# A first product on four PSUM bank pairs, half of v's first cast on GpSimd ahead of the weight loads, and two units of chunk 1 in another order

## Chip, cores, metric

One core of one Trainium2 chip. The metric is the device time of one execution in microseconds (us). The kernel before takes 262.2 to 262.4 us (median, in every set of rounds). The experiments come from three chips, one for each set of rounds, each beside runs of the kernel before on the same chip; so kernels of different sets are compared by their ratios to it.

## The reference, cut to what matters

```python
# per batch and head: q softmaxed over its 64 columns, k over its 576 rows
kv  = einsum('bhsd,bhse->bhde', k_s, v)
x   = einsum('bhsd,bhde->bhse', q_s, kv)      # -> x: 4608 x 512
h   = x @ w_in                                 # 512 -> 2048
out = (h * sigmoid(h)) @ w_out                 # 2048 -> 512
```

q, k and v are [8, 8, 576, 64], the output is 4608 x 512, all float32.

## The kernel before

Tokens go in chunks of 512 (the first product of chunk 0 takes the 576 of batch 0). In front of chunk 0 stands a short chain for batch 0: exponential, sum and normalisation of q, transposes on TensorE, exponential of k, cast of v, k times v ("kv"), the product with transposed q that gives XT, and its evacuation. The first product of chunk 0 (W1 times XT, "wide" in the code) has 16 blocks of 128 rows, each of eight matmuls of 288 columns; its result lies in a pair of PSUM banks until ScalarE (tanh) and VectorE have read it. A block can start only when its pair has been freed.

```python
    def wide_mm(fb, cs, ns=range(2)):
        for c in cs:
            for n in ns:
                nc.tensor.matmul(out=PS[:, 2 * (fb % 3) + n, 0:S // 2],   # pairs 0, 2, 4 in turn
                                 lhsT=W1[:, c, fb*128:(fb+1)*128],
                                 rhs=XTS[0][:, c, n*(S//2):(n+1)*(S//2)], ...)
```

The start of batch 0, and the order in which GpSimd issues its loads (it casts the weights to fp16 in the DMA):

```python
    exp_q(0, 0); qsum(0, 0); exp_q(0, 1)
    nc.gpsimd.tensor_copy(gate, st[0]["kt", 0][0:1, 1, 0:1])   # one element: holds the loads until k has landed
    load_w1(0, 4, 0, 2); load_w1(0, 4, 2, 4); load_w1(4, 8)
    load_w1(8, 16, 0, 2); load_w1(8, 16, 2, 4)
    load(1, "qt", ...) x2; load_w2(0, 4); load(1, "kt", ...) x2; load_w2(4, 8); load(1, "vt", ...) x2
    ...
    vcast(0, 0, nc.scalar)             # v's first half of batch 0, fp32 -> bf16
    trcopy(0, 0, 0, 5, 0, nc.scalar)   # transposed q out of PSUM
```

After the first product come units in a fixed order, the "plain" second product of chunk 0 (`mm2_plain`, "b") mixed with groups of chunk 1's first product (`group`, "g", seven products in the order 1, 2, 6, 5, 7, 4, 3). Work for other engines is tied to the number of a unit and is queued in front of it:

```python
    four_pairs = "ggbgbgbgbbgbgb"
    units += [b0.pop(0) for _ in range(9)]
    units += [{"b": b0, "g": gs}[x].pop(0) for x in four_pairs]        # b1 + 9 and on
    ...
    plan(b1 + 10, lambda: exp_q(2, 0))                                  # ScalarE
    plan(b1 + 11, lambda: (qsum(2, 0, 0), qsum(2, 0, 1), qnorm(2, 0, nc.gpsimd)))   # VectorE, GpSimd

    # in group(t, g, i), behind the matmuls:
        if i == 1:   group_snap(t, 0)     # ScalarE copies banks 0 and 1
        elif i == 2: group_add(t, 0)      # VectorE adds banks 6 and 7: group 5 writes these next
```

The softmax here doesn't subtract the row's maximum and nothing guards it: scores larger than these inputs give would overflow.

Of the kernel before, what the change touches and what calls it, by code (L numbers as in the profile page):

```python
# [17 lines left out]
def kernel(  # L18
# [9 lines left out]
    nc = tc.nc  # L28
    B, H, S, D = q.shape
# [3 lines left out]
    J = S // P  # L33
    NG = H // 2
    NC = DM // 128
# [36 lines left out]
    gate = glob.tile([1, 1], FP32, name="gate")  # L72
    dummy = glob.tile([1, 1], FP32, name="dummy")
    PS = ps.tile([128, 8, 512], FP32, name="PS")
# [10 lines left out]
    st = [dict() for _ in range(B)]  # L85

    def copy(eng, o, i):
        if eng is nc.scalar:
            eng.copy(out=o, in_=i)  # L89
        else:  # L90
            eng.tensor_copy(o, i)  # L91

    def load(b, name, src, cc, eng):
        t = ld.tile([128, 2, J * D], FP32, name=name)
        st[b][name, cc] = t
        x = src[b].rearrange("(g r) (p j) d -> g (r p) (j d)", r=2, j=J)
        eng.dma_start(out=t, in_=x.rearrange("g x y -> x g y")[:, 2 * cc:2 * cc + 2, :])

    def jgd(b, name, cc):
        return st[b][name, cc].rearrange("p g (j d) -> p j g d", d=D)  # L100
# [4 lines left out]
    def exp_q(b, cc, g0=0, g1=2):  # L105
        if "eq" not in st[b]:
            st[b]["eq"] = ap.tile([128, J, NG * D], BF16, name="eq")
        nc.scalar.activation(  # L108
            out=half(st[b]["eq"], cc)[:, :, g0:g1], in_=jgd(b, "qt", cc)[:, :, g0:g1], func=ACT.Exp
        )  # L110

    def exp_k(b, cc):
        nc.scalar.activation(out=half(ek, cc), in_=jgd(b, "kt", cc), func=ACT.Exp)  # L113

    def vcast(b, cc, eng, g0=0, g1=2):
        o = vaug[:, :, 2 * cc + g0:2 * cc + g1, 0:D]
        i = jgd(b, "vt", cc)[:, :, g0:g1, :]
        copy(eng, o, i)
# [21 lines left out]
    def qsum_end(b, cc):  # L140
        new_zq(b)
        nc.vector.reduce_sum(out=st[b]["zq"][:, cc], in_=st[b]["t2", cc], axis=AX.X)
        nc.vector.reciprocal(out=st[b]["rzq"][:, cc], in_=st[b]["zq"][:, cc])
# [16 lines left out]
    def qnorm(b, cc, eng):  # L160
        e = half(st[b]["eq"], cc)
        r = st[b]["rzq"][:, cc]
        eng.tensor_tensor(  # L163
            out=e, in0=e, in1=r[:, :, :, None].to_broadcast([128, J, 2, D]), op=ALU.mult
        )

    def new_qt(b):
        if "qT" not in st[b]:
            st[b]["qT"] = ap.tile([128, J, 2, 128], BF16, name="qT", bufs=2)
        return st[b]["qT"]  # L170
# [7 lines left out]
    def tr(b, cc, j0, j1, bank):  # L178
        t = PS[:, bank, :].bitcast(BF16)
        for j in range(j0, j1):  # L180
            nc.tensor.transpose(
                out=t[:, (j - j0) * 128:(j - j0 + 1) * 128],
                in_=st[b]["eq"][:, j, cc * 128:(cc + 1) * 128],
                identity=ident,
            )

    def trcopy(b, cc, j0, j1, bank, eng=nc.vector):
        t = PS[:, bank, :].bitcast(BF16)[:, 0:(j1 - j0) * 128].rearrange("x (j y) -> x j y", y=128)
        copy(eng, new_qt(b)[:, j0:j1, cc, :], t)

    def kv(b, cc):
        for j in range(J):
            for r in range(2):
                for s in range(2):
                    nc.tensor.matmul(  # L195
                        out=PS[s * 64:(s + 1) * 64, 6 + r, cc * 128:cc * 128 + E1],
                        lhsT=ek[r * 64:(r + 1) * 64, j, (2 * cc + s) * D:(2 * cc + s + 1) * D],
                        rhs=vaug[r * 64:(r + 1) * 64, j, 2 * cc + s, :],
                        start=(j == 0),
                        stop=(j == J - 1),  # L200
                    )
# [28 lines left out]
    def xt_mm(b, cc, col, n, bank, dst):  # L230
        for r in range(2):
            for s in range(2):
                h = slice(s * 64, (s + 1) * 64)
                nc.tensor.matmul(  # L234
                    out=PS[r * 64:(r + 1) * 64, bank + s, dst:dst + n],
                    lhsT=kvn[b % 3][h, cc, r, :],
                    rhs=st[b]["qT"][h, col // P:(col + n) // P, cc, r * 64:(r + 1) * 64],
                )

    def xt_evac(t, cc, bank, d0, d1, o0, eng):  # L240
        o = XTS[t % 2][:, 2 * cc:2 * cc + 2, o0:o0 + d1 - d0]
        copy(eng, o, PS[:, bank:bank + 2, d0:d1])
# [8 lines left out]
    def silu(t, fb, i, o, w):  # L251
        sg = mp.tile([128, S], FP32, name="sg", bufs=3)
        s = sg[:, 0:w]
        if len(i.shape) == 3:
            s = s.rearrange("p (a n) -> p a n", a=2)
        nc.scalar.activation(out=s, in_=i, func=ACT.Tanh, scale=OS)  # L256
        nc.vector.scalar_tensor_tensor(  # L257
            out=o, in0=s, scalar=1.0, in1=i, op0=ALU.add, op1=ALU.mult
        )

    def wide_mm(fb, cs, ns=range(2)):
        for c in cs:
            for n in ns:
                nc.tensor.matmul(  # L264
                    out=PS[:, 2 * (fb % 3) + n, 0:S // 2],
                    lhsT=W1[:, c, fb * 128:(fb + 1) * 128],
                    rhs=XTS[0][:, c, n * (S // 2):(n + 1) * (S // 2)],
                    start=(c == 0),
                    stop=(c == NC - 1),
                )  # L270

    def wide_silu(fb):
        bank = 2 * (fb % 3)
        silu(
            0, fb, PS[:, bank:bank + 2, 0:S // 2],
            GTS[0][:, fb, :].rearrange("p (a n) -> p a n", a=2), S,
        )
# [12 lines left out]
    def mm1(t, fb, bank):  # L290
        o0 = pieces(t)[0][3]
        mm1_mm(t, fb, bank, range(NC))
        nc.scalar.activation(
            out=GTS[t % 2][:, fb, o0:TCH], in_=PS[:, bank, o0:TCH], func=ACT.Silu, scale=1.0 / XS
        )
# [113 lines left out]
    def mm2_plain(t, fc):  # L409
        for tb in range(4):  # L410
            nc.tensor.matmul(  # L411
                out=PS[:, 2 + tb, :],
                lhsT=GTS[t % 2][:, fc, tb * 128:(tb + 1) * 128],
                rhs=W2[:, fc, :],
                start=(fc == 0),
                stop=(fc == NFB - 1),
            )
# [128 lines left out]
    def heat(n, bank=5):  # L546
        for _ in range(n):
            nc.tensor.matmul(out=PS[:, bank, :], lhsT=warm[:, 0:128], rhs=warm, start=True, stop=True)

    def load_w1(f0, f1, c0=0, c1=NC):  # L550
        nc.gpsimd.dma_start(
            out=W1[:, c0:c1, f0 * 128:f1 * 128],
            in_=w_in[c0 * 128:c1 * 128, f0 * 128:f1 * 128].rearrange("(c p) f -> p c f", p=128),
        )
# [8 lines left out]
    exp_q(0, 0)  # L563
    qsum(0, 0)
    exp_q(0, 1)
    nc.gpsimd.tensor_copy(gate, st[0]["kt", 0][0:1, 1, 0:1])
    load_w1(0, 4, 0, 2)
    load_w1(0, 4, 2, 4)
    load_w1(4, 8)
    load_w1(8, 16, 0, 2)  # L570
    load_w1(8, 16, 2, 4)
    load(1, "qt", q, 0, nc.gpsimd)
    load(1, "qt", q, 1, nc.gpsimd)
    load_w2(0, 4)
# [10 lines left out]
    tr(0, 0, 5, J, 1)  # L585
    heat(7)
    qnorm(0, 1, nc.vector)
    vcast(0, 0, nc.scalar)
    trcopy(0, 0, 0, 5, 0, nc.scalar)
    trcopy(0, 0, 5, J, 1)  # L590
    kv(0, 0)
    kvcopy(0, 0, 1)
# [3 lines left out]
    xt_mm(0, 0, 0, 320, 4, 0)  # L596
    xt_mm(0, 0, 320, 256, 0, 0)
    heat(3, 6)
    vcast(0, 1, nc.scalar, 0, 1)
    vcast(0, 1, nc.vector, 1, 2)  # L600
    trcopy(0, 1, 0, 5, 2, nc.scalar)
    trcopy(0, 1, 5, J, 3)
    kv(0, 1)
    kvcopy(0, 1, 2)
    heat(2, 3)
# [2 lines left out]
    xt_mm(0, 1, 0, 320, 6, 0)  # L608
    xt_mm(0, 1, 320, 256, 2, 0)
    wide_mm(0, (0, 1))  # L610
    xt_evac(0, 1, 6, 0, 320, 0, nc.scalar)
    xt_evac(0, 1, 2, 0, 256, 320, nc.vector)
    wide_mm(1, (0, 1))


    units = []
    at = {}

    def plan(u, f):
        at.setdefault(u, []).append(f)  # L620

    def wide(fb):
        wide_mm(fb, range(2 if fb < 2 else 0, NC))
        wide_silu(fb)

    for fb in range(NFB):
        units.append(lambda fb=fb: wide(fb))
# [17 lines left out]
    four_pairs = "ggbgbgbgbbgbgb"  # L645

    b0 = [lambda i=i: mm2_plain(0, i) for i in range(NFB)]
    gs = [lambda i=i: group(1, 1, i, None, True) for i in ORDER]
    units += [b0.pop(0) for _ in range(9)]
    units += [{"b": b0, "g": gs}[x].pop(0) for x in four_pairs]  # L650
    units += [lambda i=i: mm1(1, FB[i], i % 4) for i in range(HF)]
    assert not (b0 or gs)

# [34 lines left out]
    for t in range(2, NCH):  # L688
# [5 lines left out]
        gs = [lambda t=t, g=g, i=i: group(t, g, i) for g in (1, 0) for i in ORDER]  # L694
# [72 lines left out]
    b1 = begin[1]  # L767
# [4 lines left out]
    plan(13, lambda: (exp_q(1, 1, 1, 2), qsum_pair(1, 1), qnorm(1, 0, nc.gpsimd)))  # L772
    plan(14, lambda: (load(2, "qt", q, 0, nc.gpsimd), load(2, "qt", q, 1, nc.gpsimd)))
    plan(b1 + 2, lambda: (exp_k(1, 0), exp_k(1, 1)))
    plan(b1 + 3, lambda: (tr(1, 0, 0, 5, 6), tr(1, 0, 5, J, 7)))
    plan(b1 + 3, lambda: (trcopy(1, 0, 0, 5, 6, nc.scalar), trcopy(1, 0, 5, J, 7)))
    plan(b1, lambda: (qsum_end(1, 1), qnorm(1, 1, nc.vector)))
    plan(b1, lambda: load_w2(12, 16))
    plan(b1 + 8, lambda: nc.scalar.copy(out=GTS[1][:, :, 0:64], in_=GTS[0][:, :, TCH:S]))
# [77 lines left out]
```

## Time and profile before

| | before |
|---|---|
| time, median (range) | 262.22 us (262.09 to 262.5) |
| span in the profile | 260.3 us |
| TensorE busy | 251.4 us, 97% |
| W1's loads issued / q of batch 1 landed | 8.60 / 25.23 us |
| first product, first matmul to the next product | 15.27 to 31.72 us |
| kv of batch 1 starts / group 5 starts | 38.91 / 46.64 us |

TensorE is the bound from about 32 us to the end, so two moments serve as milestones: the start of kv of batch 1 and the start of group 5. Landing times are the last of a load's 16 landing events in the trace.

The timeline of TensorE in the kernel before (start, length, engine, line, operation; in brackets the idle time before it and what ended that): the first product, kv of batch 1, group 5 behind a plain block.

```profile
15.27 15.28 PE L264 MATMUL PS<-XT,W 128*128 128x288 f16 x120 [0.25 <-DVE XT L91]
30.74 1.14 PE L264 MATMUL PS<-XT,W 128*128 128x288 f16 x8 [0.20 <-DVE GT L257]
...
38.91 0.81 PE L195 MATMUL PS<-vaug,ek 64*64 64x65 bf16 x72
...
45.78 1.03 PE L411 MATMUL PS<-W,GT 128*128 128x512 f16 x4
46.64 0.93 PE L374 MATMUL PS<-XS,WS 128*128 128x224 f16 x8
```

The timeline of GpSimd:

```profile
7.87 0.78 POOL L566 COPY gate<-kt 1x1 f32<-1x1 f32 x1 [6.56 <-DMA kt<-in_k_dram]
8.60 3.80 POOL L551 DMA_DIRECT2D W<-in_moe_w_in_dram  x5
```

and the busy table of its early stretches (busy time of TensorE's matmuls, its weight loads, VectorE, ScalarE and GpSimd with instruction counts, then TensorE's clock, the DMA engines' busy share, GB/s; the share is the sum of the packets' times over that of 16 engines, so packets that overlap take it above 1):

```profile
11.00:12.00 1.00, 0.64 (x42) 0.53 (x28) 0.98 (x3) 1.00 (x2) 1.00 (x2) 1.00 1.20 238
12.00:13.00 1.00, 0.94 (x16) 0.42 (x14) 0.97 (x3) 0.83 (x3) 1.00 (x2) 1.00 1.20 191
13.00:14.00 1.00, 1.00 (x40) 0.53 (x39) 0.41 (x2) 1.00 (x2) 1.00 (x3) 1.00 1.11 162
```

### The profile page before, as it was taken

The numbers are of one execution on the slowest core, as the hardware profiler recorded it, in microseconds if no ns is written. First come the engines' busy times: TensorE is split into PE (matmuls) and PEld (weight loads), VectorE is DVE, ScalarE is ACT, GpSimd is POOL, SyncE is SP. The second block draws the span as 40 slices with busy tenths as digits, with TensorE's granted clock in tenths as the row PEclk, the third lists the DMA queues.
The fourth block names the chain that finished last, engine by engine and source line by source line (L and its number), as shares of the span: only waits on it lengthen the run. The fifth ranks groups of instructions, "written<-read, shape, count | busy, mean of one in ns | idle before, by whom it ended". The sixth has DMA issues, their size and how long they took to land.

```text
span 260.3 us, 6411 instructions
## 1 busy us (share of the span) xinstructions
PE 251.4 (97%) x2732; PEld 203.0 (78%) x2732; DVE 206.8 (79%) x268; ACT 187.6 (72%) x212; POOL 66.3 (25%) x63
## 2 busy tenths in 40 slices
PE   8799999999999999999999999999999999999992
PEld 3357756656888888888888888888888888888881
DVE  2957798888997999799979997999798548855832
ACT  5757887898993899489948994899473848484610
POOL 1753791640351205030502060306000000000003
PEclk9999999999999999999999999999999999999999
DMA  7999999689989485958694869630443004300624
GB/s 256 342 193 299 303 329 331 237 181 390 306 306 254 108 248 189 240 119 223 213 256 107 229 209 193 166 75 3 91 87 77 3 0 88 76 3 1 141 63 121
DMA packets 35452, 45.89 MB, mean 176 GB/s; under 512 B 16208, under 2 KB 19984, under 8 KB 35424
## 3 DMA queue, kind: packets, MB, share of 16 engines
q1 hardware_dynamic: 29568, 33.69, 47.6%
q0 software_dynamic: 5616, 11.60, 16.9%
q8 instruction: 21, 0.34, 0.5%
q10 hardware_dynamic: 240, 0.20, 0.2%
q14 instruction: 7, 0.06, 0.1%
HBM read 36.70 MB, written 9.44 MB: 177 GB/s over the span
## 4 chain that ended last, share of the span: by engine, by line
PE 88%; DVE 4%; ACT 2%; POOL 2%; DMA 1%; issue 1%; POOLq 0%; ACTq 0%
PE PS L474 37%; PE PS L374 35%; PE PS L411 5%; PE PS L264 3%; PE PS L282 2%; PE PS L234 2%; PE PS L195 2%; DMA qt<-in_q_dram 1%; DVE eq L163 1%; DVE zq L154 1%; ACT sg L256 1%; POOL out_dram L736 1%; ACT eq L108 1%; DVE GT L257 1%; POOL h L132 0%
## 5 line engine op out<-in xcount | busy, mean ns | idle before, releaser
L352 DVE TENSOR_TENSOR h<-PS,h 128x1024 f32<-128x1024 f32 (+1 forms) x45 | 54.0, 1199 | 13.0 <-ACT h L89 6.8
L474 PEld LDWEIGHTS <-GT 128*128 128x128 f16 x512 | 49.5, 98 | 6.9 <-issue 1.2
L374 PEld LDWEIGHTS <-WS 128*128 128x128 f16 x480 | 46.8, 98 | 6.4 <-issue 0.4
L474 PE MATMUL PS<-W,GT 128*128 128x256 f16 x384 | 49.1, 273 | 0.0
L374 PE MATMUL PS<-XS,WS 128*128 128x256 f16 (+1 forms) x360 | 46.3, 272 | 0.0
L358 ACT ACTIVATE GT<-h 128x1024 f16<-128x1024 f32 (+1 forms) x45 | 46.1, 1047 | 0.3 <-DVE h L352 0.3
L89 ACT COPY h<-PS 128x1024 f32<-128x1024 f32 (+1 forms) x35 | 35.1, 1003 | 13.4 <-PE PS L374 12.9
L163 POOL TENSOR_TENSOR eq<-eq,rzq 128x1152 bf16<-128x1152 bf16 x13 | 27.7, 2133 | 53.8 <-DVE rzq L158 53.4
L474 PEld LDWEIGHTS <-S 128*128 128x128 f16 x384 | 37.2, 98 | 5.2 <-issue 1.0
L374 PEld LDWEIGHTS <-W 128*128 128x128 f16 x360 | 34.7, 98 | 4.8 <-issue 0.5
L474 PE MATMUL PS<-T,S 128*128 128x256 f16 x256 | 32.7, 273 | 0.0
L374 PE MATMUL PS<-XT,W 128*128 128x256 f16 (+1 forms) x240 | 29.5, 272 | 0.1
L358 ACT ACTIVATE GT<-PS 128x1024 f16<-128x1024 f32 (+1 forms) x15 | 15.2, 1016 | 18.9 <-PE PS L374 18.9
L91 POOL CAST vaug<-vt 128x1152 bf16<-128x1152 f32 x12 | 14.8, 1239 | 43.3 <-DMA vt<-in_v_dram 43.3
L736 POOL DMA_DIRECT2D out_dram<-ow x5 | 2.7, 546 | 72.5 <-DVE ow L721 72.5
L108 ACT ACTIVATE eq<-qt 128x1152 bf16<-128x1152 f32 (+1 forms) x18 | 19.0, 1057 | 2.5 <-DMA qt<-in_q_dram 2.5
L154 DVE TENSOR_REDUCE zq<-eq 128x18 f32<-128x1152 bf16 x12 | 16.1, 1346 | 3.8 <-ACT eq L108 3.8
L113 ACT ACTIVATE ek<-kt 128x1152 bf16<-128x1152 f32 x16 | 18.3, 1153 | 0.8 <-DMA kt<-in_k_dram 0.8
L264 PE MATMUL PS<-XT,W 128*128 128x288 f16 x128 | 16.4, 286 | 0.5 <-DVE XT L91 0.2
L474 PE MATMUL PS<-W,S 128*128 128x256 f16 x128 | 16.5, 273 | 0.0
L494 DVE SCALAR_TENSOR_TENSOR ow<-PS,sc 128x512 f32<-128x512 f32 x7 | 4.8, 692 | 14.5 <-ACT sc L490 14.5
L264 PEld LDWEIGHTS <-W 128*128 128x128 f16 x128 | 12.4, 98 | 4.4 <-issue 1.3
(79 smaller groups left out, 345.4 us busy)
## 6 DMA issues: line engine op xcount, KB each, us to landing
out_dram<-ow SPq DMA_DIRECT2D x64, 128.0 KB, 2.4
qt<-in_q_dram SPq DMA_DIRECT2D x12, 576.0 KB, 4.7
kt<-in_k_dram SPq DMA_DIRECT2D x12, 576.0 KB, 5.7
vt<-in_v_dram SPq DMA_DIRECT2D x12, 576.0 KB, 5.4
qt<-in_q_dram POOLq DMA_DIRECT2D x4, 576.0 KB, 10.5
kt<-in_k_dram POOLq DMA_DIRECT2D x4, 576.0 KB, 13.9
vt<-in_v_dram POOLq DMA_DIRECT2D x4, 576.0 KB, 12.9
W<-in_moe_w_out_dram POOLq DMA_DIRECT2D x4, 512.0 KB, 15.0
```

What stands on the lines that cost most here:

```text
L89: eng.copy(out=o, in_=i)
L91: eng.tensor_copy(o, i)
L108: nc.scalar.activation(out=half(st[b]["eq"], cc)[:, :, g0:g1], in_=jgd(b, "qt", cc)[:, :, g0:g1], func=ACT.Exp)
L113: nc.scalar.activation(out=half(ek, cc), in_=jgd(b, "kt", cc), func=ACT.Exp)
L154: nc.vector.reduce_sum(out=z, in_=e, axis=AX.X)
L163: eng.tensor_tensor(out=e, in0=e, in1=r[:, :, :, None].to_broadcast([128, J, 2, D]), op=ALU.mult)
L264: nc.tensor.matmul(out=PS[:, 2 * (fb % 3) + n, 0:S // 2], lhsT=W1[:, c, fb * 128:(fb + 1) * 128], rhs=XTS[0][:, c, n * (S // 2):(n + 1) * ...
L352: nc.vector.tensor_tensor(out=four(t, i), in0=group_bank(t, True), in1=four(t, i), op=ALU.add)
L358: nc.scalar.activation(out=group_out(t, f, n), in_=x, func=ACT.Silu, scale=1.0 / XS)
L374: nc.tensor.matmul(out=PS[:, bank + p // 2, (p % 2) * HT:(p % 2) * HT + width(t)], lhsT=a[:, c, p * 128:(p + 1) * 128], rhs=bb[:, c, 0:wid ...
L411: nc.tensor.matmul(out=PS[:, 2 + tb, :], lhsT=GTS[t % 2][:, fc, tb * 128:(tb + 1) * 128], rhs=W2[:, fc, :], start=(fc == 0), stop=(fc == N ...
L474: nc.tensor.matmul(out=PS[:, bank, m * HN:(m + 1) * HN], lhsT=a[:, fc, m * 128:(m + 1) * 128], rhs=bb[:, fc, :], start=(first and fc == 0) ...
```

## The change

Its intent: the first product starts without waiting for VectorE's evacuation and turns on four bank pairs, so that it does not wait for ScalarE and VectorE; half of v's first cast moves from ScalarE to GpSimd and takes the place of the gate; copies of transposed q go ahead of casts of v; one plain block goes between groups 1 and 2, where TensorE waited for XT.

```diff
+    WIDE = (4, 0, 2, 6) * 3 + (4, 2, 0, 6)
+    def wide_mm(fb, cs):
+        for n in range(2):
+            for c in cs:
-                    out=PS[:, 2 * (fb % 3) + n, 0:S // 2],
+                    out=PS[:, WIDE[fb] + n, 0:S // 2],
...
-    nc.gpsimd.tensor_copy(gate, st[0]["kt", 0][0:1, 1, 0:1])
+    vcast(0, 0, nc.gpsimd, 1, 2)
...
-    load_w1(8, 16, 0, 2)
-    load_w1(8, 16, 2, 4)
+    load_w1(8, 12)
+    load_w1(12, 16)
...
-    vcast(0, 0, nc.scalar)
     trcopy(0, 0, 0, 5, 0, nc.scalar)
+    vcast(0, 0, nc.scalar, 0, 1)
...
+    trcopy(0, 1, 5, J, 3)
     vcast(0, 1, nc.scalar, 0, 1)
     vcast(0, 1, nc.vector, 1, 2)
     trcopy(0, 1, 0, 5, 2, nc.scalar)
-    trcopy(0, 1, 5, J, 3)
...
     wide_mm(1, (0, 1))
+    wide_mm(2, (0, 1))
...
-    units += [{"b": b0, "g": gs}[x].pop(0) for x in four_pairs]
+    units += [{"b": b0, "g": gs}[x].pop(0) for x in "gbggbgbgbbgbgb"]
...
-    plan(b1 + 3, ...)   # transposes of batch 1's q and their copies
+    plan(b1 + 4, ...)
```

More of the change, by code (lines that the diff above doesn't have):

```diff
@@ L259, in silu @@
         )
-    def wide_mm(fb, cs, ns=range(2)):
-        for c in cs:
-            for n in ns:
+    WIDE = (4, 0, 2, 6) * 3 + (4, 2, 0, 6)
+    def wide_mm(fb, cs):
+        for n in range(2):
+            for c in cs:
                 nc.tensor.matmul(
-                    out=PS[:, 2 * (fb % 3) + n, 0:S // 2],
+                    out=PS[:, WIDE[fb] + n, 0:S // 2],
                     lhsT=W1[:, c, fb * 128:(fb + 1) * 128],
@@ L272, in wide_silu @@
     def wide_silu(fb):
-        bank = 2 * (fb % 3)
+        bank = WIDE[fb]
         silu(
@@ L622, in wide @@
     def wide(fb):
-        wide_mm(fb, range(2 if fb < 2 else 0, NC))
+        wide_mm(fb, range(2 if fb < 3 else 0, NC))
         wide_silu(fb)
@@ L774 @@
     plan(b1 + 2, lambda: (exp_k(1, 0), exp_k(1, 1)))
-    plan(b1 + 3, lambda: (tr(1, 0, 0, 5, 6), tr(1, 0, 5, J, 7)))
-    plan(b1 + 3, lambda: (trcopy(1, 0, 0, 5, 6, nc.scalar), trcopy(1, 0, 5, J, 7)))
+    plan(b1 + 4, lambda: (tr(1, 0, 0, 5, 6), tr(1, 0, 5, J, 7)))
+    plan(b1 + 4, lambda: (trcopy(1, 0, 0, 5, 6, nc.scalar), trcopy(1, 0, 5, J, 7)))
     plan(b1, lambda: (qsum_end(1, 1), qnorm(1, 1, nc.vector)))
```

## The prediction

> **What bounds the kernel now.** I read the page first, then the busy table by stretches, then the timelines of each engine in the first 60 us, where all the changed code lies.
>
> From the page of the kernel before, the busy slices of the TensorE and its granted clock:
>
> ```profile
> PE   8799999999999999999999999999999999999992
> ...
> PEclk9999999999999999999999999999999999999999
> ```
>
> TensorE is busy all through at full clock, 251.4 of 260.3 us. By stretches it is 50.00 of 50 us between 100 and 150 us and again between 150 and 200. So nothing after about 60 us can win back or absorb anything: whatever moment TensorE reaches there, the end moves with it. What can change is the start, and the waits of TensorE in the first 60 us. Listing the starts of its matmuls, these are the places where it steps further than its rhythm (0.1225 us for a 288-column matmul of the first product, eight of them a block, 0.98 us): 0.13 us at 15.63, 0.22 at 18.21, 0.07 at 28.23, 0.36 at 30.26 (the sum, 0.78 us, is all that the first product loses between 15.27 and 31.72), then 0.2 at 41.8 and 0.29 at 43.1. That is 1.3 us in all, and the change goes for each of them.
>
> ScalarE in the second half of the first product:
>
> ```profile
> 24.63 0.65 ACT L256 ACTIVATE sg<-PS 128x576 f32<-128x576 f32 x1 [0.33 <-PE PS L264]
> 25.25 0.68 ACT L108 ACTIVATE eq<-qt 128x576 bf16<-128x576 f32 x1
> 25.84 0.63 ACT L256 ACTIVATE sg<-PS 128x576 f32<-128x576 f32 x1
> 26.37 0.67 ACT L108 ACTIVATE eq<-qt 128x576 bf16<-128x576 f32 x1
> 26.95 1.28 ACT L256 ACTIVATE sg<-PS 128x576 f32<-128x576 f32 x2
> 28.12 0.68 ACT L108 ACTIVATE eq<-qt 128x576 bf16<-128x576 f32 x1
> 28.69 0.64 ACT L256 ACTIVATE sg<-PS 128x576 f32<-128x576 f32 x1
> ```
>
> The exponential of batch 1's q stands between the tanh of blocks 8 and 9. Its q lands at 25.23 (the last of the 16 landing events of that load), and the exponential starts at 25.25: the load has no slack. From there ScalarE has no idle time, and through VectorE it sets when PSUM banks come free.
>
> VectorE and ScalarE where the first two groups of chunk 1 are multiplied:
>
> ```profile
> 43.98 0.39 DVE L335 TENSOR_TENSOR XS<-XT,XS 128x448 f16<-128x448 f16 x1
> 44.42 1.09 DVE L352 TENSOR_TENSOR h<-PS,h 128x896 f32<-128x896 f32 x1
> 45.43 1.40 DVE L156 TENSOR_REDUCE zq<-eq 128x9 f32<-128x576 bf16 x2
> 46.87 0.27 DVE L158 RECIPROCAL rzq<-zq 128x18 f32<-128x18 f32 x1
> ```
>
> ```profile
> 42.43 0.91 ACT L89 CAST XT<-PS 128x896 f16<-128x896 f32 x1 [0.48 <-PE PS L234]
> 43.35 0.91 ACT L89 COPY h<-PS 128x896 f32<-128x896 f32 x1
> 44.15 1.17 ACT L108 ACTIVATE eq<-qt 128x1152 bf16<-128x1152 f32 x1
> ```
>
> The line to hold on to is L352, which reads the result of group 2 out of banks 6 and 7. Group 5 writes those banks next, at 46.64, and does not wait now, as L352 is done at 45.51, ahead of the two sums of q.
>
> **What the Trainium skill says.** "PSUM — Partial Sum Buffer", Engine vs sequencer instructions, has it that the queues of ScalarE, VectorE and GpSimd are strict FIFO and that matmuls keep program order. Nothing in the trace contradicts it, and it is why an instruction put earlier in VectorE's queue can hold up another that is ready. "SBUF — State Buffer", Who interferes with whom, says that a VectorE instruction with two SBUF inputs and a GpSimd instruction that reads SBUF exclude each other, and that a reduction never does. The trace agrees: the one-element copy ahead of W1's loads took 0.78 us, from 7.87 to 8.65, under a two-input product on VectorE that ended at 8.61, while the other such copy took 0.18 us. "DMA: Bandwidth & Descriptors", Why a DMA increments its semaphore by 16 and not by 1, says that 16 engines finish independently and only the 16th shows that all has landed. The trace agrees: for v's second half of batch 0 fourteen landing events lie between 11.39 and 11.87, the last two at 12.23 and 12.30.
>
> **The change, part by part.**
>
> *Half of v's cast on GpSimd, W1's loads behind it.* The cast waits for v at 9.32. Whole casts take 1.16 us (1152 columns) when undisturbed; with the 0.18 us of a one-element copy as fixed part I estimate 0.67 us for the half, so 9.38 to 10.05, beside a reduction on VectorE (8.53 to 9.88) and finished before the two-input product at 10.21. W1's first load is thus issued at about 10.0 in place of 8.60. That is not 1.4 us of DMA: the engines are still on q, k and v until 11.4 to 11.9, two of them until 12.3. A GpSimd store at the end had its first packet 0.58 us after its issue ended (253.50 plus 0.59 to 254.67); so W1's would start near 10.0 + 0.87 + 0.58 = 11.45. The engines that finish early lose up to half a microsecond, the late ones, which post the last landing, little. I take 0.1 us. The two last loads are now 1024-byte rows for all four row blocks: such a load of W1 took 2.77 us from first landing to first landing (14.01 to 16.78), the two with 2048-byte rows 2.48 and 2.53; I take 0.1 us more for each. In all, loads behind W1 come 0.3 us later. I call this d; it could be 0 to 0.8. The stream is saturated to 45 us (DMA share above 1.0 there), so d carries on.
>
> *Copies of transposed q ahead of casts of v.* On VectorE the copy (0.41) and cast (0.76) change places between 12.32 and 13.40; kv's second half waits for the cast, 13.08 before and 13.43 now, but it started at 13.48 behind filler matmuls anyway. On ScalarE v's second half lands at 12.30, as before. Worth 0. The chain on VectorE from 5.56 to 12.30 has no gap and is not shortened.
>
> *The first product on four bank pairs.* Its first matmul needs no longer the evacuation of bank 0 on VectorE, but of bank 4 on ScalarE (done 14.18): it starts right behind the last product, 14.95 for 15.27, does two matmuls, then waits to 15.27 for the other columns. With 126 matmuls left and the waits at 15.63 and 18.21 gone, block 4 is reached at 15.27 + 30 x 0.1225 = 18.94 (its W1 lands at 18.73 + 0.1: just in time), block 13 at 27.76. Block 13 uses the pair of block 10, as it did before, and block 10 is freed behind the exponential that waits for q: tanh at 26.97 + d, VectorE until 28.38 + d. So block 13 starts at 28.43 + d, where it started before (28.43). Blocks 14 and 15 no longer wait: the end is 28.43 + 3 x 0.98 = 31.37 + d for 31.72. Of the 0.78 us, 0.35 - d arrive. d = 0.3: 0.05.
>
> *Transposes of batch 1 one unit later.* They are reached at 31.4 + 3.45 = 34.85 + d, GpSimd's normalisation ends at 34.29: no wait. Kv of batch 1 is reached at 38.6 + d (38.91 before); its v lands at 37.77 + d and its cast takes 0.76: ready at 38.6 + d. So 0.3 - d, or about 0, is left.
>
> *"gbgg" for "ggbg".* The second group waited until 43.39 for the evacuation of XT (ends 43.34). A block of the plain product (0.86 us) goes before it: the 0.29 us are filled. But the sums of q of batch 2 are tied to the unit's number, and the second group has moved from the tenth unit to the eleventh. The order of VectorE in the built program shows it: four XS differences, two sums of q, reciprocal, and only then L352's addition. The sums wait for ScalarE's exponential, which ends at 45.32 as before. So: sums 45.34 to 46.76, reciprocal, addition from 46.96 (0.18 after the reciprocal starts, as the next instruction did) for 1.09 to 48.05, group 5 at 48.10. TensorE is there at 42.32 + 0.78 + 0.86 + 0.77 + 0.77 + 0.86 = 46.36 and stands for 1.74 us. Against 46.64 before, that is a loss of 1.46 us, the filled gap already counted.
>
> *Sum:* 1.46 - (0.3 - d) = 1.16 + d, with d = 0.3: 1.46. Nothing later gives it back: 262.22 + 1.4 = 263.6 us, rounded.
>
> **The rivals.** First, the addition costs nothing, as the exponential comes earlier too, or the tool's order misleads: then the kernel gains 0.3 - d and the filled 0.29, giving 261.6 to 262.0. For it speaks the intent of the change; against it that the exponential follows ScalarE's copy (43.35 to 44.26) without a gap, and that copy hangs on evacuations moved by no part of the change. Second, W1 arrives late: block 4 has 0.1 us of slack, and if the first packets come 2.3 us after issue, as W1's did before (8.60 to 10.89, though behind q, k and v), every load comes up to 0.8 us later, and the wait at 38.6 passes it on: 264.2. Third, GpSimd's cast runs longer and holds VectorE's product at 10.21: a cast of 1.2 us would give 0.4 us at the start, but block 13's wait for q swallows most. Fourth, the bank waits really were the cost and all 0.78 us plus the start arrive: 261.2 without the addition's wait, 262.7 with it; q's landing speaks against it.
>
> **Range and chances.** The two terms are 1.46 (I trust the order; its length to 0.2 us) and d - 0.3 (-0.4 to +0.5). That makes 262.7 to 264.3. Runs of the kernel before differ by 0.4 us. Two per cent is 5.2 us, and no rival comes near: 0.98 for within 2%.
>
> **What would show it.** A wait of group 5 on VectorE's addition of about 1.7 us near 46 to 48, with sums of q ahead of it; block 13 starting near 28.4 to 28.9 behind VectorE; the first product beginning near 14.95 and ending near 31.4 to 31.9; q of batch 1 landing at 25.2 to 26; W1's issue near 10.0. I am wrong if group 5 does not wait, or if TensorE stands at block 4 or at kv of batch 1 for over half a microsecond.

## The result, and the profile after

265.30 us median (264.56 to 265.86, four runs), 262.36 for the kernel before beside them. The ratio is 1.0111 [1.0079, 1.0144]: slower by 2.9 us, inside 2%, but outside the range of the prediction. Ratios here and below are the mean time of one kernel's fast runs over the mean of the other's fast runs of the same rounds, so not quite the ratio of the medians quoted.

| | before | predicted | after (profile) |
|---|---|---|---|
| W1's loads issued | 8.60 | 10.0 | 9.64 |
| first product starts | 15.27 | 14.95 | 14.98 |
| q of batch 1 landed | 25.23 | 25.5 | 26.65 |
| block 13 starts | 28.43 | 28.7 | 29.85 |
| kv of batch 1 starts | 38.91 | 38.9 | 39.96 |
| group 5 starts | 46.64 | 48.1 | 49.44 |
| from kv to group 5 | 7.73 | 9.2 | 9.48 |
| span | 260.3 | | 263.1 |

Group 5 is 2.80 us late, and so is the end (263.1 - 260.3 = 2.8): 1.05 us lost by kv of batch 1, and 1.75 us between there and group 5.

The page of the kernel after, TensorE's slices; the eighth digit, an 8 where a 9 stood, is the second of the two losses:

```profile
PE   8889899799999999999999999999999999999992
```

The timeline of VectorE of the kernel after, at the place that the prediction showed:

```profile
45.04 0.38 DVE L338 TENSOR_TENSOR XS<-XT,XS 128x448 f16<-128x448 f16 x1
46.72 1.42 DVE L156 TENSOR_REDUCE zq<-eq 128x9 f32<-128x576 bf16 x2 [1.30 <-ACT eq L108]
48.17 0.27 DVE L158 RECIPROCAL rzq<-zq 128x18 f32<-128x18 f32 x1
48.36 1.03 DVE L355 TENSOR_TENSOR h<-PS,h 128x896 f32<-128x896 f32 x1
```

and of TensorE, kv of batch 1 and the group that waits for the addition:

```profile
39.96 0.81 PE L195 MATMUL PS<-vaug,ek 64*64 64x65 bf16 x72
...
46.55 1.03 PE L414 MATMUL PS<-W,GT 128*128 128x512 f16 x4
...
49.44 0.93 PE L377 MATMUL PS<-XS,WS 128*128 128x224 f16 x8 [1.86 <-DVE h L355]
```

The addition (L355 now, L352 before) had its operands when group 2 was done, at about 46 us, but stands in VectorE's queue behind two sums that wait 1.30 us for ScalarE's exponential. Group 5 waits for the addition. That is the prediction's mechanism. From matmul start to matmul start the step is 2.24 us where 0.22 is the rhythm.

The first loss is in the loads. GpSimd, and the same stretches of the busy table:

```profile
9.02 0.68 POOL L91 CAST vaug<-vt 128x576 bf16<-128x576 f32 x1 [7.71 <-DMA vt<-in_v_dram]
9.64 3.85 POOL L554 DMA_DIRECT2D W<-in_moe_w_in_dram  x5
```

```profile
11.00:12.00 1.00, 0.64 (x42) 0.53 (x31) 1.00 (x3) 0.70 (x2) 1.00 (x3) 1.00 0.71 140
12.00:13.00 1.00, 0.94 (x16) 0.43 (x14) 0.93 (x4) 1.00 (x2) 1.00 (x3) 1.00 1.12 133
13.00:14.00 1.00, 1.00 (x40) 0.53 (x39) 0.46 (x1) 0.83 (x2) 1.00 (x2) 1.00 0.90 120
```

From 11 to 12 us the DMA engines are busy 0.71 for 1.20, and in the next two microseconds they move 133 and 120 GB/s for 191 and 162. W1's later loads, then the loads of batch 1, come that much later, and ScalarE and TensorE wait for them:

```profile
26.67 0.68 ACT L108 ACTIVATE eq<-qt 128x576 bf16<-128x576 f32 x1 [0.83 <-DMA qt<-in_q_dram]
```

```profile
17.34 11.74 PE L267 MATMUL PS<-XT,W 128*128 128x288 f16 x92 [0.71 <-DMA W<-in_moe_w_in_dram]
29.85 3.10 PE L267 MATMUL PS<-XT,W 128*128 128x288 f16 x24 [0.77 <-DVE GT L257]
```

The exponential of q, before which ScalarE did not stand idle in the kernel before, now waits 0.83 us for q; and W1's second load (17.29 for 14.96) holds the first product, which the prediction had not seen at all. Block 13's start has moved by 29.85 - 28.43 = 1.42 us, exactly as far as q's landing (26.65 - 25.23). Behind it block 15 no longer waits (0.36 us before), and 1.05 of the 1.42 us are left at kv of batch 1. TensorE does not wait for v there: its step into kv is 0.31 us in both profiles.

### The profile page after: what moved, and what is told of

It is laid out like the page before. It is cut to its first block, busy times and chain, and to the rows that moved or that the text cites. A ratio compares the mean times of both kernels' runs of the same rounds, so it can differ in the third digit from the quotient of the medians.

```text
span 263.1 us, 6410 instructions
## 1 busy us (share of the span) xinstructions
PE 252.0 (96%) x2732; PEld 203.1 (77%) x2732; DVE 208.7 (79%) x268; ACT 187.1 (71%) x212; POOL 66.0 (25%) x63
## 4 chain that ended last, share of the span: by engine, by line
PE 83%; DMA 6%; issue 4%; POOL 2%; ACT 2%; DVE 2%; POOLq 0%; ACTq 0%
PE PS L477 36%; PE PS L377 34%; DMA qt<-in_q_dram 5%; PE PS L414 5%; PE PS L285 2%; PE PS L234 2%; PE PS L195 2%; PE PS L267 1%; POOL W L554 1%; POOL out_dram L740 1%; ACT eq L108 1%; DMA W<-in_moe_w_in_dram 1%; DVE zq L156 1%; ACT sg L256 0%; PE PS L181 0%
## 5 line engine op out<-in xcount | busy, mean ns | idle before, releaser
L355 DVE TENSOR_TENSOR h<-PS,h 128x1024 f32<-128x1024 f32 (+1 forms) x45 | 53.9, 1197 | 12.2 <-ACT h L89 6.3
L91 POOL CAST vaug<-vt 128x1152 bf16<-128x1152 f32 (+1 forms) x13 | 15.5, 1197 | 51.9 <-DMA vt<-in_v_dram 51.2
L497 DVE SCALAR_TENSOR_TENSOR ow<-PS,sc 128x512 f32<-128x512 f32 x7 | 4.8, 691 | 14.5 <-ACT sc L493 14.5
```

The lines of the kernel that those rows point to most:

```text
L91: eng.tensor_copy(o, i)
L355: nc.vector.tensor_tensor(out=four(t, i), in0=group_bank(t, True), in1=four(t, i), op=ALU.add)
```

## The experiments

Two theories to begin with. A: 1.75 us is the addition behind the sums. B: the rest is the later issue of W1's loads. Fourteen profiles in all; their milestones first, in us from the start of the span:

| kernel | W1 issued | first 500 KB, after issue | q of batch 1, after issue | kv of batch 1 | kv to group 5 | median | ratio |
|---|---|---|---|---|---|---|---|
| before | 8.60 | 5.46 | 16.63 | 38.91 | 7.73 | 262.2 | |
| after | 9.64 | 5.71 | 17.01 | 39.96 | 9.48 | 265.30 | 1.0111 |
| after_again | 12.50 | 5.56 | 16.37 | 42.18 | 9.48 | 266.44 | 1.0154 |
| undo_swap | 10.30 | 5.65 | 17.11 | 40.71 | 7.73 | 263.56 | 1.0053 |
| late_sums | 10.44 | 5.28 | 16.15 | 39.90 | 7.44 | 263.65 | 1.0051 |
| early_w1 | 8.61 | 5.66 | 16.51 | 38.43 | 9.16 | 263.06 | 1.0035 |
| both | 8.55 | 5.77 | 16.53 | 38.39 | 7.45 | 261.60 | 0.9978 |
| gate_v | 9.90 | 5.65 | 16.49 | 39.71 | 7.45 | 262.91 | 1.0020 |
| gate_q | 6.10 | 8.48 | 19.18 | 39.76 | 7.45 | 262.84 | 1.0022 |
| both_split | 8.65 | 6.12 | 16.95 | 38.92 | 7.45 | 261.95 | 0.9981 |
| both_3pairs | 8.68 | 5.60 | 17.15 | 39.47 | 7.45 | 262.53 | 1.0003 |
| before_swap | 8.52 | 5.95 | 16.04 | 38.85 | 9.16 | 263.46 | 1.0053 |
| before_cast | 10.72 | 5.57 | 16.39 | 40.74 | 7.74 | 264.40 | 1.0080 |
| both_oldcopies | 8.58 | 5.50 | 16.37 | 38.26 | 7.45 | 261.65 | 0.9978 |

"First 500 KB" is when the packets of GpSimd's queue had moved 500 KB (as written, in fp16), counted from the issue of W1's first load. All results were correct, and each kernel was timed in five rounds (the kernel after at first in fewer).

### undo_swap and late_sums: the addition

```diff
# undo_swap: the changed kernel with
-    ... for x in "gbggbgbgbbgbgb"]
+    ... for x in four_pairs]
# late_sums: the changed kernel with
-    plan(b1 + 11, lambda: (qsum(2, 0, 0), qsum(2, 0, 1), qnorm(2, 0, nc.gpsimd)))
+    plan(b1 + 12, lambda: (qsum(2, 0, 0), qsum(2, 0, 1), qnorm(2, 0, nc.gpsimd)))
```

> The changed kernel with the two units of chunk 1 back in their old order (group 1, group 2, block of the plain product). Theory A (half of the loss, 1.75 us of 2.8, is VectorE's addition of group 2 standing behind the two sums of q, so that group 5 waits): the wait of group 5 is gone, the step before it is 0.1 us in place of 2.24, a wait of 0.3 us before group 2 is back, and the time falls from 265.3 by about 1.75 us to 263.5. Rival (whatever was late at 40 us, a load, would hold TensorE a little later all the same, and the swap only shows where): the wait moves, and the time stays within 0.4 us of 265.3.

> The changed kernel, its new order of units kept, but the two sums of q and their reciprocal planned one unit later, behind the addition. Theory A: the wait of group 5 is gone and the filled gap in front of group 2 stays filled, so about 0.3 us better than with the old order: 263.2 us. Rival 1 (the sums are needed early: GpSimd's normalisation of q and kv of batch 2 behind them come too late): a new wait at kv of batch 2, and 264 or more. Rival 2 (the swap is harmless): 265.3.

Measured: 263.56 us (ratio 1.0053) and 263.65 us (1.0051), for 1.0111 of the kernel after. In both the wait of group 5 is gone. VectorE in late_sums, the addition ahead of the sums again:

```profile
45.99 1.09 DVE L355 TENSOR_TENSOR h<-PS,h 128x896 f32<-128x896 f32 x1 [0.63 <-PE PS L377]
46.99 1.40 DVE L156 TENSOR_REDUCE zq<-eq 128x9 f32<-128x576 bf16 x2
```

So theory A holds for the cause. Its worth comes to 1.5 to 1.7 us here, but loads were not equally late in the runs compared; before_swap gives the cleaner size. The gap that the swap was meant to fill shows in the profiles alone (7.44 us from kv to group 5 in late_sums, 7.73 in undo_swap); in the times the two are equal, as loads came differently late in them: W1's second load held the first product by 1.9 us in undo_swap's profile, by 0.1 in that of late_sums, whose third load then held it by 0.8.

### before_swap: the same loss with no load late

```diff
# the kernel before with
-    ... for x in four_pairs]        (chunk 1's first list)
+    ... for x in "gbggbgbgbbgbgb"]
```

> The kernel before with nothing changed but the order of units (group 1, block of the plain product, group 2). Theory A: no load is late here, so this is the 1.46 us of the prediction's own working: group 5 starts 9.1 to 9.2 us after kv of batch 1 in place of 7.73, and the time is 263.6 to 263.7 us, ratio 1.0055. Rival (the wait only appears when loads are late): ratio 1.000, or 0.999 with the filled gap.

Measured: 263.46 us, ratio 1.0053 [1.0040, 1.0066]. TensorE in its profile:

```profile
45.44 1.03 PE L411 MATMUL PS<-W,GT 128*128 128x512 f16 x4
48.01 0.93 PE L374 MATMUL PS<-XS,WS 128*128 128x224 f16 x8 [1.54 <-DVE h L352]
```

Group 5 starts 9.16 us after kv for 7.73: a loss of 1.43 us, where the prediction worked out 1.46. The rival (only late loads make the wait) falls.

In the kernel after it was 1.75. The difference of 0.32 us is ScalarE's copy of group 1's banks, which is in front of the exponential: it starts 0.33 us after XT's evacuation ends (44.39 to 44.72), where the kernel before leaves 0.01. This delay stands in all five profiles of kernels with the cast on GpSimd and in none of the nine others. What causes it is open.

### early_w1 and both: the loads

```diff
# early_w1: the changed kernel with
-    vcast(0, 0, nc.gpsimd, 1, 2)
+    nc.gpsimd.tensor_copy(gate, st[0]["kt", 0][0:1, 1, 0:1])
...
-    vcast(0, 0, nc.scalar, 0, 1)
+    vcast(0, 0, nc.scalar)
# both: early_w1 and late_sums together
```

> The changed kernel, but the gate of before (a one-element copy on k's landing) in front of W1's loads and all of v's first half cast on ScalarE, behind transposed q. Theory B (the other 1.05 us of the loss is that W1's loads are issued 1.04 us later, and the whole stream of GpSimd's loads with them): issue at 8.6, the q of batch 1 lands at about 25.4 in place of 26.65, v's second half of batch 1 at about 37.9 in place of 38.85, TensorE reaches kv of batch 1 at about 38.8 in place of 39.96, and the time falls by about 1.05 us to 264.2. Rival (the loads are slower for their 1024-byte rows, or for the copies' new order, not for their issue): q of batch 1 lands no more than 0.4 us earlier and the time stays above 264.9.

> Both of these at once: the sums one unit later, and W1's loads behind the gate of before. Theories A and B together: 265.3 - 2.05 - 1.05 = 262.2 us, or 0.2 to 0.5 us below the kernel before, as the bank pairs and the swap then earn what is left of their intent (0.3 us each, if q of batch 1 lands as early as before). If the two losses share a cause (whoever waits first hides the other), less than 2.5 us come back and the time is above 262.8.

Measured: early_w1 263.06 us (1.0035), which is 2 us better than after by the ratios, twice what was expected; both 261.60 us, ratio 0.9978 [0.9966, 0.9990], better than the kernel before. The two corrections add up: 0.0060 from late_sums and 0.0076 from early_w1 make 0.0136, and both gives 1.0111 - 0.9978 = 0.0133. They do not hide each other, as far as two measurements of the kernel after allow (the second, below, gave 1.0154).

The excess over 1.05 us has two sources that I can name: kv of batch 1 starts at 38.43, 1.53 us before the profile of after, and earlier than before's 38.91, as TensorE now earns the four bank pairs; and the 0.32 us of ScalarE's copy are gone. A third is that the profile of after was a mild case, as the next run shows.

### after_again: the changed kernel once more

No edit.

> The changed kernel, unaltered, on this chip, beside the others of this call. Its four runs so far lie between 264.56 and 265.86 us. If the loss is made of the two parts that the runs so far show (addition 1.5 to 1.75 us, W1's issue 1 to 2 us), the ratio to before is 1.009 to 1.012, and W1's issue lies between 9.6 and 10.5 us, where v's first half has landed and its cast of 0.68 us is done.

Measured: 266.44 us (265.51 to 267.27), ratio 1.0154 [1.0134, 1.0174], outside what I expected; W1's issue at 12.50. The kernel before spread over 0.6 us beside it, this one over 1.8. The timelines of VectorE and GpSimd in its profile:

```profile
10.36 0.27 DVE L158 RECIPROCAL rzq<-zq 128x18 f32<-128x18 f32 x1
10.66 1.36 DVE L163 TENSOR_TENSOR eq<-eq,rzq 128x1152 bf16<-128x1152 bf16 x1
```

```profile
10.79 1.76 POOL L91 CAST vaug<-vt 128x576 bf16<-128x576 f32 x1 [9.48 <-DMA vt<-in_v_dram]
12.50 3.85 POOL L554 DMA_DIRECT2D W<-in_moe_w_in_dram  x5
```

In this execution v's first half landed at 10.74, not at 8.97. The cast then began 0.13 us after a VectorE product with two SBUF inputs and took 1.76 us for 0.68, ending 0.5 us after that product (12.02). This is the exclusion of "SBUF — State Buffer", Who interferes with whom, met from GpSimd's side; the trace agrees, 0.68 us without such a product and 1.76 with it. So the cast in front of the loads does not just delay them, it ties them to a landing that moves by over 1 us between executions (8.97 to 10.74 in the fourteen profiles; the profile of after has the earliest, which is luck) and to a port that is taken from 10.2 or 10.7 us on. The gate of before has the same two ties, but to an earlier landing and an earlier product, and ends near 8.6 whether k has landed at 7.8 (0.78 us under the product) or later (0.18 us):

```profile
8.49 0.18 POOL L569 COPY gate<-kt 1x1 f32<-1x1 f32 x1 [7.18 <-DMA kt<-in_k_dram]
8.61 3.86 POOL L554 DMA_DIRECT2D W<-in_moe_w_in_dram  x5
```

(that is early_w1). In the profile of after_again the later cast also held kv of batch 0, by 0.79 us. That did not reach the first product, whose start waited another 1.10 us for W1's first load (landed 17.44; the first matmul started at 17.49).

### before_cast: the cast alone

```diff
# the kernel before with
-    nc.gpsimd.tensor_copy(gate, st[0]["kt", 0][0:1, 1, 0:1])
+    vcast(0, 0, nc.gpsimd, 1, 2)
-    vcast(0, 0, nc.scalar)
+    vcast(0, 0, nc.scalar, 0, 1)
```

> The kernel before with half of v's first cast on GpSimd ahead of W1's loads in place of the one-element copy, the other half on ScalarE, and nothing else changed. Theory B: issue at 9.7 to 10.4 in place of 8.60, all of GpSimd's loads later by as much, v of batch 1 too, whose cast leaves TensorE 0.36 us of slack at kv: 0.7 to 1.4 us lost there, 262.9 to 263.6 us, ratio 1.003 to 1.005. Rival, the prediction's own (the engines are still on q, k and v, so a later issue costs 0.1 us): ratio under 1.001.

Measured: 264.40 us (263.45 to 265.54), ratio 1.0080 [1.0061, 1.0100], more than theory B expected, and far from the prediction's 0.1 us. In its profile issue is at 10.72, q of batch 1 lands at 27.11, kv of batch 1 starts at 40.74, 1.83 us late. The parts add up to the first measurement of the whole: 0.0080 for the cast, 0.0053 for the swap, -0.0022 for what both has left (pairs, order of transposes and loads, swap with late sums) make 0.0111, the ratio of the kernel after. That it fits to the last digit is chance: the second measurement gave 0.0154 (after_again).

Here the cast (10.10 us) began ahead of VectorE's product with two SBUF inputs (10.27), and it was the product that took longer, 1.71 us for 1.36 (1.62 in late_sums, 1.47 in undo_swap). The first product began at 15.68 for 15.27, but W1's second load, which landed at 17.84, held it anyway.

### gate_v and gate_q: when the loads are issued

```diff
# gate_v: both with
-    nc.gpsimd.tensor_copy(gate, st[0]["kt", 0][0:1, 1, 0:1])
+    nc.gpsimd.tensor_copy(gate, st[0]["vt", 0][0:1, 1, 0:1])
# gate_q: both with
+    nc.gpsimd.tensor_copy(gate, st[0]["qt", 1][0:1, 1, 0:1])
```

> The kernel of the run both (sums one unit later, all of v's first half cast on ScalarE), with the one-element copy ahead of W1's loads waiting on the landing of v's first half in place of k's. Nothing is cast on GpSimd in front of the loads: only their issue is later, by about 1.2 us less the 0.6 us of copy under VectorE's product that the gate on k needs. Theory B (the moment of issue decides, the cast matters through its duration alone): issue at 9.4 to 9.9, q of batch 1 lands at issue + 16.5 = 26, and the time lies between both (261.6) and late_sums (263.65): 262.6 to 263.1. Rival (the cast on GpSimd itself slows the stream, by its port): as fast as both, within 0.4 us.

> The same kernel with the copy ahead of W1's loads waiting on the second half of q of batch 0, which lands at 5.9. Theory C (the stream of GpSimd's loads is paced, over the first microseconds after its issue, by the loads' own preparation, and the DMA engines wait for it between 11.5 and 14.5): issue near 6.0, the engines find work ready as q, k and v end, no dip of their busy share, q of batch 1 lands 0.7 to 1.5 us earlier than in both (25.08), block 13 hardly waits, and the time is 261.1 to 261.4. Rival 1 (the loads then share the engines with k and v of batch 0, whose landings set the start): v's halves land over 0.5 us later and the time is 262 or more. Rival 2 (the engines' rate alone sets the landings): q of batch 1 lands as in both and so does the time.

gate_v: 262.91 us, ratio 1.0020 [1.0001, 1.0039], as theory B expected: issue at 9.90, q of batch 1 at 26.39. With nothing cast on GpSimd the later issue alone costs 0.0042 over both, 1.1 us; the cast on top of it (late_sums, issued 0.54 us later still in its profile, and measured in another set) 0.0031 more.

gate_q: 262.84 us, ratio 1.0022 [1.0001, 1.0044]. What theory C forecast does not come. Issued at 6.10, the stream's first packet moved at 10.27 only, and from there it shared the engines with v's last load of batch 0, which landed at 14.62 for 12.67 in both. ScalarE in gate_q:

```profile
11.46 1.16 ACT L113 ACTIVATE ek<-kt 128x1152 bf16<-128x1152 f32 x1 [0.39 <-DMA kt<-in_k_dram]
14.64 0.67 ACT L89 CAST vaug<-vt 128x576 bf16<-128x576 f32 x1 [2.02 <-DMA vt<-in_v_dram]
```

The first product started near 16.9 for 15.0, and q of batch 1 landed no earlier than in both (25.28 for 25.08): rival 1. Of the three moments tried the gate on k is the best: the earlier one takes from v, the later one leaves the engines idle.

What the column of the table shows: in the thirteen profiles with issue at 8.5 us or later, 500 KB had moved 5.3 to 6.1 us after issue and q of batch 1 had landed 16.0 to 17.2 us after it, whether the engines still had batch 0's loads to do at first (issue at 8.6) or stood idle (12.50). The second 500 KB took 2.5 to 2.9 us. The mean for q is 16.6 us in the seven profiles with issue near 8.6 and in the six later ones. So in this range the first half megabyte follows its issue, and a later issue is passed on in full, give or take half a microsecond. In gate_q it does not: there 500 KB had moved at 14.58 us, no earlier than in both (14.32). What paces the start, the preparation of the transfers on GpSimd or something else, no run here shows; GpSimd's five issuing instructions took 3.8 to 3.9 us together in all fourteen.

### both_split, both_3pairs, both_oldcopies: the other parts

```diff
# both_split: both with
-    load_w1(8, 12); load_w1(12, 16)
+    load_w1(8, 16, 0, 2); load_w1(8, 16, 2, 4)
# both_3pairs: both with
-    WIDE = (4, 0, 2, 6) * 3 + (4, 2, 0, 6)
+    WIDE = (0, 2, 4) * 5 + (0,)
# both_oldcopies: both with v's casts ahead of the copies of transposed q, as before, on ScalarE and VectorE
```

> The kernel of the run both with W1's last two loads cut as before (two row blocks of all eight blocks' columns, 2048-byte rows) in place of four row blocks of four. The prediction charged 0.2 us for the shorter rows. If that is right, q of batch 1 lands 0.1 to 0.3 us earlier and the time is 261.3 to 261.6; but block 8 needs the second of these loads at about 23.3 us where it lands at about 23.5, so a wait of 0.2 to 0.6 us at block 8 may come, which the waits at block 13 would hide. Rival: the shorter rows cost 0.5 us or more, and the time falls below 261.2.

> The kernel of the run both with the first product on three bank pairs again (0, 2, 4 in turn). If the four pairs are worth what the prediction says (0.35 us at the end of the first product, where block 15 no longer waits, the rest being hidden by block 13's wait), waits come back near 18 and at block 15, and the time is 261.9 to 262.1. If their worth is all of the 0.78 us of waits, 262.4; if nothing of it reaches the end, 261.6.

> The kernel of the run both with the casts of v ahead of the copies of transposed q again, on ScalarE and on VectorE. The prediction gives this part no worth, as filler matmuls hold kv of batch 0 to 13.48 in either order: first product's start within 0.1 us, ratio within 0.001 of that of both (0.9978). Rival (ScalarE's second exponential of k and its evacuation start sooner with the copies first): 0.3 us slower or more.

both_split: 261.95 us, ratio 0.9981 for 0.9978: no difference, where I expected up to 0.3 us less. The wait has moved from block 13 to block 8 (a step of 0.85 us at 23.29), as expected, and the shorter rows cost 0.1 us at most (W1's third load to q of batch 1: 6.42 us for 6.52).

both_3pairs: 262.53 us, ratio 1.0003, 0.65 us slower than both, where I expected 0.3 to 0.5. Waits come back at blocks 1, 3, 13 and 15 (0.14, 0.71, 0.10, 0.36 us). Not a clean price: with three blocks begun ahead, block 3's wait is 0.71 us where the kernel before had 0.22, and q of batch 1 landed 0.76 us later in this profile. The four pairs are worth something like half a microsecond here; how much of it is theirs is not shown.

both_oldcopies: 261.65 us, ratio 0.9978 [0.9967, 0.9990]: the order of copies and casts is worth nothing, as predicted.

## Why the prediction was wrong, point by point

1. **The addition behind the sums: right.** Named from the built order, sized at 1.46 us; before_swap measured 1.43. In the kernel after it came to 1.75, with 0.32 us of a copy on ScalarE that starts late in every kernel with the cast on GpSimd, cause open.
2. **d, the lateness of the loads: the step that failed.** The prediction said "That is not 1.4 us of DMA: the engines are still on q, k and v", took 0.1 us for the issue and 0.2 for the rows, and set d = 0.3. d measured 1.42 at q of batch 1 and 1.08 at v of batch 1; of the 1.42, 1.04 is the later issue, and 0.38 lies within the spread of landings after issue. The issue (10.0 for 9.64) and the first packet (11.45 for 11.22) were predicted well for this profile (the five kernels with the cast issue at 9.64 to 12.50); what failed is the thought that a later issue costs only the time in which engines stand idle, as if a stream ran at once at their rate. The first 500 KB took about as long from issue as before (5.71 us for 5.46). The dip at 13.5 to 14.5 us in the kernel before stood in a query made ahead of the prediction and was not followed up; it was the sign: no other queue had work left for the engines, and the stream moved 131 and 127 GB/s. gate_v, where only the issue is later, shows the cost without the cast: 1.1 us.
3. **How d acts: right.** Block 13 at 28.43 + d and kv at 38.6 + d were the formulas; with q's d of 1.42 they give 29.85 (measured 29.85) and 40.02 (39.96). v's d of 1.08 would allow kv at 39.68, so v was not what held it. With d = 1.42 the prediction's own sum, 1.16 + d, is 2.58 us, and 0.32 us of ScalarE's copy make 2.90 for the 2.8 in the profile.
4. **Block 4 "just in time": wrong with d.** W1's second load was the first to be missed (0.88 us at 16.34), its third held block 4 by 0.29 us; block 13's wait for q hid both. The second rival had forecast loads up to 0.8 us late and 264.2 us, nearer than the main line, but by a first packet 2.3 us after issue; it came after 1.58.
5. **The third rival, a longer cast on GpSimd, was weighed from one side only.** I asked what the cast could do to VectorE's product. That came in three of the five profiles with the cast (1.47 to 1.71 us for 1.36), ahead of waits for W1's loads. In after_again the product held the cast, and by it the loads, which I had not asked. The margin that I stated, 10.05 against 10.21, was 0.16 us, less than the landing of v moves between executions.
6. **Copies ahead of casts, and rows: right**, nothing and 0.1 us. The start at 14.95 came at 14.98.

## What to carry to other kernels

An instruction tied to a place in one engine's order moves in another engine's queue when that order changes; look for what it now stands in front of, and whether its operands are there. A load stream that must be full when others end has to be issued ahead of that by its own start-up time, but not so early that it takes from loads that are needed first (in gate_q v landed 1.95 us later than in both); do not put work that depends on a late landing in front of its issue. Of the change, both kept what was good, with the cast undone, the gate put back and the sums moved by one unit: 261.6 us, ratio 0.9978 to the kernel before.

## What the Trainium skill lacked or had wrong

- "DMA: Bandwidth & Descriptors", Latency and other measured facts, gives about 1 us to the first byte of a load issued by GpSimd, and not from where it counts. The first packet moved 1.56 to 1.58 us after the start of the issuing instruction, 0.7 us after its end, in the six profiles where the engines were about to run dry (2.2 to 2.6 us after the start in the seven with issue near 8.6). No page has the start of a stream of several casting loads: 5.3 to 6.1 us from issue to the first 500 KB, 2.5 to 2.9 us for the next.
- The same page, Issuing engines are not separate DMA queues, says that loads of all engines interleave. In gate_q they do, from 10.27 us on, but the first packet came 4.17 us after issue, while the engines were on SP's loads; the page has nothing on such a delay.
- "SBUF — State Buffer", Who interferes with whom, was borne out: a cast of 0.68 us took 1.76 us when it began 0.13 us after a VectorE product with two SBUF inputs; begun 0.17 us ahead of it (before_cast), it kept its 0.68 us and the product took 1.71 us for 1.36.
- No page has ScalarE's 0.33 us between the end of one evacuation and the start of the next copy, seen in five profiles of fourteen (0.01 us in the others).
